# Products of an expert layer summed in two PSUM banks

## The chip, the cores and the metric

The kernel runs on one core of one Trainium2 chip. The metric is the device time of one execution in microseconds (us); lower is better. The engines are PE (TensorE: matrix products into PSUM; PEld is its weight load), DVE (VectorE), ACT (ScalarE), POOL (GpSimd) and SP (SyncE, which here issues DMAs). Each engine works off its own queue in order, and engines wait for each other through semaphores.

## The reference

```
attention:  for each of 768 steps:  y = r . state
            state = state * w - outer(state . a, b) + outer(v, k)        (4 x 8 heads of 40)
x = y as 3072 tokens x 320
mixture:    P = exp(x @ w_gate - max)           (3072 x 8)
            8 times:  P /= rows' sums;  P /= columns' sums;  P *= 3072 / 8
            for e in 0..7:  out += P[:, e] * (relu(x @ w1[e]) @ w2[e])   (w1: 320 x 1024, w2: 1024 x 320)
```

## The kernel before

The first 500 us compute the attention in chunks. The rest, which the change is about, is the mixture of experts, in 128 blocks. One block takes one expert, 768 of the 3072 tokens (four groups, held two at a time) and 256 of the 1024 hidden columns. Eight blocks in a row make up one expert for two token groups (two groups of four); all experts are gone through once for groups 0 and 1 and then, backwards, for groups 2 and 3. The PE works on fp32 numbers split into a high and a low part.

**First layer of a block (`layer1`).** The 2 x 2 block product is done with seven products instead of eight (`PROD`), each of 128 x 384 outputs and four matmuls (`product`). A product is written into one of two PSUM banks, `pl[0]` and `pl[1]`, that alternate: product j+2 can start only when product j has been read. In order they are 1, 2, 5, 6, 3, 7, 4 (`ORDER`). From them come two hidden tiles `sm0`, `sm1`, each with two halves of 384 tokens (`h1`, `h2`), through seven additions on VectorE (`add`), with two copies on ScalarE (`p1`, `p5`). Four times a half is then rectified by ScalarE (`relu`, high part `hh`), and VectorE computes the remainder max(sm, 0) - hh (`low`, low part `hl`). The last remainders of a block (`rest`) stand in the queues after the first product of the next block.

**Second layer (`layer2`).** Twelve units a block of three matmuls (128 x 320 outputs, into six banks `op0` to `op5`), which wait in `pend` and are put between the products of the next block: two after each of the first five products, one after each of the last two, three units behind (`LAG`). After the fourth block of a token group (`f == FP - 1`), `evac` moves each `op` bank out: a VectorE operation for most experts.

**Work beside it.** Each product is a slot. After each slot one step of `background` is put in the queues: `prep_w` splits the weights of a coming block (four ScalarE casts, nine GpSimd operations, lines 514 to 532), four preparations in each run of eight blocks; `prep_x` splits the tokens. `sinkhorn` computes the gate P in the first ten blocks: a step of it every few slots (`S_GAP`), with a matmul into one of the two `pl` banks each.

**Order.** Up to block 7 (`N_MAN = 8`) a scheduler with a timeline model orders the instructions; from block 8 on they stand in each queue as they were written.

Of the kernel before, what the change touches and what calls it, by code (L numbers as in the profile page):

```python
# [23 lines left out]
E, FF, DM = 8, 1024, 320  # L24
# [423 lines left out]
SC = 2  # L448
NT = 6
S_WAIT = 2  # L450
S_GAP = 5
LAG = 3
N_MAN = 8
D_WAIT = 6
ORDER = (1, 2, 5, 6, 3, 7, 4)
PROD = {1: (0, 0), 2: (1, 2), 3: (6, 1), 4: (2, 6), 5: (3, 3), 6: (4, 4), 7: (5, 5)}


# [1 line left out]
def body(ctx, tc, d, out):  # L460
    nc = tc.nc
# [5 lines left out]
    pmat = one.tile([128, 24, E], F32, name="pmat")  # L467
# [19 lines left out]
    pl = [ctx.enter_context(tc.tile_pool(name=f"pl{i}", bufs=1, space=bass.MemoryType.PSUM)) for i in range(2)]  # L487
# [77 lines left out]
                        op=ALU.subtract)  # L565
        yield

    def product(o, i, k, s):
        ia, ib = PROD[i]
        wh = whs[k % NWS][:, 640:2432].rearrange("r (i k m) -> r i k m", k=2, m=128)  # L570
        wl = wls[k % NWS][:, 640:1536].rearrange("r (i m) -> r i m", m=128)
        xh, xl = xch[s % SC], xcl[s % SC]
        ts = [(wh[:, ia, 0], xh[:, ib, 0]), (wh[:, ia, 0], xl[:, ib]), (wl[:, ia], xh[:, ib, 0]),
              (wh[0:96, ia, 1], xh[0:96, ib, 1])]
        for j, (w_, x_) in enumerate(ts):
            nc.tensor.matmul(o, lhsT=w_, rhs=x_, start=(j == 0), stop=(j == 3))  # L576

    def layer1(n, k, s):
        h1, h2 = slice(384, 768), slice(0, 384)
        v = nc.vector  # L580
        hh = hp.tile([128, 2, 768], F32R, name="hh")
        hl = hp.tile([128, 2, 768], F32R, name="hl")

        sm = [hp.tile([128, 768], F32, name=f"sm{i}", bufs=1) for i in range(2)]
        p1, p5, u2, u3 = (hp.tile([128, 384], F32, name=x, bufs=1) for x in ("p1", "p5", "u2", "u3"))

        def prod(i):
            j = (n + ORDER.index(i)) % 2
            o = pl[j].tile([128, 512], F32, name=f"p{i}", tag="pl")[:, 0:384]
            product(o, i, k, s)  # L590
            return o

        def add(out, x, y, eng=nc.vector):
            eng.tensor_tensor(out=out, in0=x, in1=y, op=ALU.add)  # L594

        def relu(f, h):
            nc.scalar.activation(out=hh[:, f, h], in_=sm[f][:, h], func=AF.Relu)  # L597

        def low(f, h):
            v.scalar_tensor_tensor(out=hl[:, f, h], in0=sm[f][:, h], scalar=0.0, in1=hh[:, f, h],  # L600
                                   op0=ALU.max, op1=ALU.subtract)

        nc.scalar.copy(out=p1, in_=prod(1))
        yield 2
        add(sm[0][:, h1], prod(2), p1)
        relu(0, h1)
        yield 2
        nc.scalar.copy(out=p5, in_=prod(5))
        low(0, h1)
        yield 2  # L610
        add(u2, prod(6), p1)
        yield 2
        add(p1, prod(3), p5)
        add(sm[0][:, h2], p1, u2)
        yield 2
        add(u3, prod(7), u2)
        relu(0, h2)
        add(sm[1][:, h2], p5, u3)
        yield 1
        add(sm[1][:, h1], prod(4), u3)  # L620
        low(0, h2)
        relu(1, h1)
        yield 1

        def rest():
            relu(1, h2)
            yield
            low(1, h1)
            low(1, h2)

        yield hh, hl, rest()

    def layer2(e, k, s, f, hh, hl):
        wh, wl = whs[k % NWS], wls[k % NWS]
        last = f == FP - 1

        def unit(h, i):
            cw = slice(h * DM, h * DM + DM)
            cs = slice(i * 128, i * 128 + 128)
            for j, (a, w_) in enumerate(((hh, wh), (hh, wl), (hl, wh))):  # L640
                nc.tensor.matmul(ops[i], lhsT=a[:, h, cs], rhs=w_[:, cw],  # L641
                                 start=(f == 0 and h == 0 and j == 0), stop=(last and h == 1 and j == 2))
            if last and h:
                evac(e, s, i)
            if h and i == 2 and s % SC == SC - 1 and k + NWS < NK and (s >= SC or e < E - 1):
                bg[0][0].append(prep_w(k + NWS))

        tiles = (3, 4, 5, 0, 1, 2)
        if last:
            return [partial(unit, h, i) for i in tiles for h in range(2)]  # L650
        return [partial(unit, h, i) for h in range(2) for i in tiles]

    def sinkhorn():
        v = nc.vector
        mxs = one.tile([128, 8], F32, name="mxs")
        mx, m1, mbs = mxs[:, 0:1], mxs[0:1, 1:2], mxs[:, 2:3]
        v.tensor_reduce(out=mx, in_=lg, op=ALU.max, axis=AX.XY)
        for _ in range(S_GAP):
            yield
        t = pl[0].tile([128, 512], F32, name="mp", tag="pl")[0:1, 0:128]  # L660
        nc.tensor.transpose(t, mx, ident)
        v.tensor_reduce(out=m1, in_=t, op=ALU.max, axis=AX.X)
        for _ in range(S_GAP):
            yield
        t = pl[1].tile([128, 512], F32, name="mb", tag="pl")[:, 0:1]
        nc.tensor.matmul(t, lhsT=ones[0:1], rhs=m1, start=True, stop=True)
        v.tensor_copy(out=mbs, in_=t)
        v.tensor_scalar(out=lg, in0=lg, scalar1=mbs, scalar2=None, op0=ALU.subtract)
        nc.scalar.activation(out=pmat, in_=lg, func=AF.Exp)
        for _ in range(S_GAP):  # L670
            yield
        rs = one.tile([128, 24], F32, name="rs")
        cl = one.tile([128, E], F32, name="cl")
        cs = one.tile([128, E], F32, name="cs")
        for i in range(8):
            v.tensor_reduce(out=rs, in_=pmat, op=ALU.add, axis=AX.X)
            v.tensor_scalar(out=rs, in0=rs, scalar1=EPS, scalar2=None, op0=ALU.add)
            v.reciprocal(out=rs, in_=rs)
            v.tensor_tensor(out=pmat, in0=pmat, in1=rs.unsqueeze(2).broadcast_to([128, 24, E]), op=ALU.mult)
            v.tensor_reduce(out=cl, in_=pmat.rearrange("p n e -> p e n"), op=ALU.add, axis=AX.X)  # L680
            for _ in range(S_GAP):
                yield
            t = pl[i % 2].tile([128, 512], F32, name="cp", tag="pl")[:, 0:E]
            nc.tensor.matmul(t, lhsT=ones, rhs=cl, start=True, stop=True)
            v.tensor_scalar(out=cs, in0=t, scalar1=EPS, scalar2=float(E) / NTOK, op0=ALU.add, op1=ALU.mult)  # L685
            v.reciprocal(out=cs, in_=cs)
            v.tensor_tensor(out=pmat, in0=pmat, in1=cs.unsqueeze(1).broadcast_to([128, 24, E]), op=ALU.mult)
            yield
        for i in range(NT):
            scale_acc(0, i)  # L690
            yield

    def scale_acc(s, i):
        nc.scalar.activation(out=acc[:, s * NT + i], in_=acc[:, s * NT + i], func=AF.Copy,
                             scale=pmat[:, s * NT + i, 0:1])

    def evac(e, s, i):
        n, m = s * NT + i, (s % SC) * NT + i
        if e == (0 if s < SC else E - 1):
            if s == 0:  # L700
                nc.scalar.copy(out=acc[:, m], in_=ops[i])
            else:
                nc.scalar.activation(out=acc[:, m], in_=ops[i], func=AF.Copy, scale=pmat[:, n, e:e + 1])
        else:
            nc.vector.scalar_tensor_tensor(out=acc[:, m], in0=ops[i], scalar=pmat[:, n, e:e + 1],
                                           in1=acc[:, m], op0=ALU.mult, op1=ALU.add)
# [16 lines left out]
    bg = [(deque(), deque()) for _ in range(2)]  # L723
    bg[0][0].extend(prep_w(k) for k in range(2, NWS))
    bg[1][0].extend(prep_x(1, u) for u in range(3))
    sink = sinkhorn()

    def background(slot):
        for new, act in bg:
# [8 lines left out]
    for n, (k, e, s, f) in enumerate(blocks):  # L738
# [92 lines left out]
```

## Time and profile before

| | |
|---|---|
| time of three runs | 1835.61 us median (1833.37 to 1836.29) |
| the profiled execution | 1835.4 us from the first to the last instruction |
| PE busy | 1732.4 us, 94% |
| DVE, ACT, POOL busy | 1360.2, 856.3, 873.2 us (74%, 47%, 48%) |
| 505 to 620 us (the first blocks) | PE busy 104.89 of 115 us, DVE 98.16 |
| 700 to 1800 us | PE busy 1100.00 of 1100 us, granted clock 1.00, DVE 816.16, ACT 444.91, POOL 518.43 |

The profiled execution lies 0.2 us below the median. A row of a group reads: line, engine, operation, output <- inputs by the program's names, shapes, count, busy us, mean ns of one, idle time before. A row of a timeline reads: start us, duration us, engine, line, operation, and in brackets an idle time before it with what ended it. Names like `p`, `sm`, `hl`, `hh` stand without their numbers there: `p<-p,p` on DVE is the sum of product 3 and the copy `p5`.

### The profile page before, as it was taken

How to read it: one execution, taken by the hardware profiler on the slowest of the kernel's cores; microseconds unless marked ns; L12 is line 12 of the kernel's file. 1: busy time of each engine (PE TensorE's matmuls, PEld its weight loads, DVE VectorE, ACT ScalarE, POOL GpSimd, SP SyncE). 2: the span in 40 equal slices, each digit the busy share in tenths (PEclk: the TensorE clock that was granted, in tenths of full speed). 3: DMA queues.
4: the chain of work that ended last, by engine and by line, in shares of the span. 5: the costliest groups of instructions: out<-in, count | busy, mean ns of one | idle time of the engine just before them, and what ended most of it. 6: DMA issues, size and time to landing. Idle time of an engine off the chain costs nothing.

```text
span 1835.4 us, 31595 instructions
## 1 busy us (share of the span) xinstructions
PE 1732.4 (94%) x11843; PEld 1703.2 (93%) x11843; DVE 1360.2 (74%) x2354; ACT 856.3 (47%) x1848; POOL 873.2 (48%) x849
## 2 busy tenths in 40 slices
PE   4479988999989999999999999999999999999999
PEld 4468888889889999999999999999999999999999
DVE  6876967866688868777776868977686877777676
ACT  6347767655743533434253434345343343425342
POOL 6545745631662626446281735007182644628160
PEclk8569999889899999999999999999999999999999
DMA  7567888875720101111020202201020111102001
GB/s 187 124 149 181 185 172 197 174 162 134 201 82 22 57 20 56 38 38 57 19 75 5 72 21 73 72 1 57 20 75 20 56 38 38 57 20 75 10 30 44
DMA packets 193303, 142.79 MB, mean 78 GB/s; under 512 B 141438, under 2 KB 170750, under 8 KB 193150
## 3 DMA queue, kind: packets, MB, share of 16 engines
q1 hardware_dynamic: 189469, 135.03, 28.4%
q10 hardware_dynamic: 3680, 5.74, 1.2%
q8 instruction: 94, 1.54, 0.3%
q14 instruction: 60, 0.48, 0.1%
HBM read 113.90 MB, written 26.82 MB: 77 GB/s over the span
## 4 chain that ended last, share of the span: by engine, by line
PE 79%; DVE 8%; DMA 5%; issue 2%; ACT 2%; POOL 2%; SPq 1%; DVEq 0%; POOLq 0%; ACTq 0%
PE op L641 36%; PE p L576 33%; DMA inp<-in_inp_dram 3%; PE xc L291 2%; PE pu L302 2%; PE av L283 1%; PE c L309 1%; PE ll L154 1%; DVE pr L188 1%; DMA td<-nd 1%; PE gp L256 1%; DVE q L119 1%; DVE hl L600 1%; PE op L261 1%; DVE sm L594 1%
## 5 line engine op out<-in xcount | busy, mean ns | idle before, releaser
L576 PE MATMUL p<-xch,wh 128*128 128x384 f32 (+1 forms) x1792 | 605.0, 339 | 5.9 <-DVE cs L685 1.8
L597 ACT ACTIVATE hh<-sm 128x384 fp32r<-128x384 f32 x512 | 269.4, 526 | 722.8 <-DVE sm L594 722.8
L641 PE MATMUL op<-wh,hh 128*128 128x320 f32 x1536 | 476.5, 311 | 2.1 <-ACT hh L597 2.1
L641 PE MATMUL op<-wl,hh 128*128 128x320 f32 x1536 | 474.2, 309 | 0.0
L641 PE MATMUL op<-wh,hl 128*128 128x320 f32 x1536 | 467.1, 310 | 2.1 <-DVE hl L600 2.1
L522 POOL TENSOR_TENSOR wl<-ws,wh 128x640 fp32r<-128x640 f32 x60 | 102.8, 1713 | 606.1 <-ACT wh L520 605.8
L600 DVE SCALAR_TENSOR_TENSOR hl<-sm,hh 128x384 fp32r<-128x384 f32 x512 | 372.6, 761 | 2.4 <-ACT hh L597 2.0
L576 PEld LDWEIGHTS p<-xch,wh 128*128 128x128 f32 (+1 forms) x1792 | 337.3, 188 | 9.8 <-DVE sm L594 3.3
L576 PE MATMUL p<-xcl,wh 128*128 128x384 f32 x896 | 302.6, 338 | 0.0
L576 PE MATMUL p<-xch,wl 128*128 128x384 f32 x896 | 301.8, 337 | 0.0
L641 PEld LDWEIGHTS op<-wh,hh 128*128 128x128 f32 x1536 | 289.9, 189 | 3.0 <-ACT hh L597 3.0
L641 PEld LDWEIGHTS op<-wl,hh 128*128 128x128 f32 x1536 | 290.7, 189 | 0.0
L641 PEld LDWEIGHTS op<-wh,hl 128*128 128x128 f32 x1536 | 286.8, 188 | 2.5 <-DVE hl L600 2.4
L594 DVE TENSOR_TENSOR sm<-p,u 128x384 f32<-128x384 f32 x384 | 234.7, 621 | 8.8
L576 PEld LDWEIGHTS p<-xcl,wh 128*128 128x128 f32 x896 | 168.7, 188 | 0.0
L576 PEld LDWEIGHTS p<-xch,wl 128*128 128x128 f32 x896 | 168.6, 188 | 0.0
L594 DVE TENSOR_TENSOR sm<-p,p 128x384 f32<-128x384 f32 x128 | 71.3, 557 | 128.5 <-PE p L576 72.1
L594 DVE TENSOR_TENSOR p<-p,p 128x384 f32<-128x384 f32 x128 | 71.1, 556 | 101.1 <-PE p L576 100.7
L594 DVE TENSOR_TENSOR u<-p,p 128x384 f32<-128x384 f32 x128 | 70.8, 553 | 57.0 <-PE p L576 55.7
L530 POOL TENSOR_TENSOR wl<-ss,wh 128x512 fp32r<-128x512 f32 x60 | 89.8, 1496 | 30.3 <-ACT wh L527 26.2
L154 PE MATMUL ll<-ab,kb 104*128 104x128 f32 x336 | 62.6, 343 | 39.5 <-POOL ab L149 14.8
L154 PEld LDWEIGHTS ll<-ab,kb 104*128 104x128 f32 x336 | 54.0, 243 | 45.1 <-POOL kb L142 27.0
(161 smaller groups left out, 2739.9 us busy)
## 6 DMA issues: line engine op xcount, KB each, us to landing
ws<-in_wts_dram SPq DMA_DIRECT2D x60, 832.0 KB
inp<-in_inp_dram SPq DMA_DIRECT2D x42, 419.2 KB
rb<-in_r_dram SPq DMA_DIRECT2D x48, 208.0 KB
ld<-lt ACTq DMA_DIRECT2D x40, 128.0 KB
gd<-g SPq DMA_DIRECT2D x48, 105.6 KB
gl<-gd SPq DMA_DIRECT2D x48, 105.6 KB
vz<-in_v_dram SPq DMA_DIRECT2D x48, 104.0 KB
xd<-y SPq DMA_DIRECT2D x24, 208.0 KB
```

The lines of the kernel that those rows point to most:

```text
L119: nc.vector.tensor_tensor_scan(out=qr.rearrange("r p t -> r (p t)"), data0=w65[:, 260:0:-1], data1=one65, initial=0.0, op0=ALU.mult, op1=A ...
L154: nc.tensor.matmul(ll[:, p], lhsT=kb[:, p], rhs=ab[:, p], start=True, stop=True)
L188: nc.vector.tensor_tensor(out=prv, in0=a.unsqueeze(2).broadcast_to([nu, n_c, n_r, n_k]), in1=m.unsqueeze(1).broadcast_to([nu, n_c, n_r, n_ ...
L291: nc.tensor.matmul(xc[h][:, p], lhsT=pp["sx"][:, p, h], rhs=f[:, p, h], start=True, stop=True)
L302: nc.tensor.matmul(pu[:, p], lhsT=tts[c][:, b * NP + p], rhs=x1[:, p], start=True, stop=True)
L522: g.tensor_tensor(out=wl[:, 0:640], in0=raw[:, 256:896], in1=wh[:, 0:640], op=ALU.subtract)
L530: g.tensor_tensor(out=lv[:, 3:7], in0=so[:, :, 0], in1=hv[:, 3:7, 0], op=ALU.subtract)
L576: nc.tensor.matmul(o, lhsT=w_, rhs=x_, start=(j == 0), stop=(j == 3))
L594: eng.tensor_tensor(out=out, in0=x, in1=y, op=ALU.add)
L597: nc.scalar.activation(out=hh[:, f, h], in_=sm[f][:, h], func=AF.Relu)
L600: v.scalar_tensor_tensor(out=hl[:, f, h], in0=sm[f][:, h], scalar=0.0, in1=hh[:, f, h], op0=ALU.max, op1=ALU.subtract)
L641: nc.tensor.matmul(ops[i], lhsT=a[:, h, cs], rhs=w_[:, cw], start=(f == 0 and h == 0 and j == 0), stop=(last and h == 1 and j == 2))
```

## The change

Products are taken in the order 1, 2, 6, 5, 7, 3, 4. Two banks `pa` and `pb` are taken once a block. Product 1 starts `pa`; products 6, 7 and 4 are added to it by the PE (`first=False`: no start flag), so that it holds in turn p1, u2 = p1 + p6, u3 = u2 + p7 and at last the whole h1 half of `sm1`. Product 2 uses `pb`, then product 5 starts it afresh and product 3 is added. ScalarE copies p1, u2, p5 and u3 out (four copies instead of two). VectorE does three additions instead of seven. The h1 half of `sm1` is never stored: ScalarE rectifies it from PSUM, and its remainder (`low(1, h1, pa)`, in `rest`) reads `pa` too. In blocks with f > 0, `layer2` takes the first six units in the order 0 to 5. `sinkhorn` does one iteration a block; its matmul goes into columns 384 to 511 of `pb`, ahead of the third product. All twelve `acc` tiles of the first expert are scaled later (`scale_acc`), and their `evac` is a plain copy.

```diff
-            nc.tensor.matmul(o, lhsT=w_, rhs=x_, start=(j == 0), stop=(j == 3))
+            nc.tensor.matmul(o, lhsT=w_, rhs=x_, start=(first and j == 0), stop=(j == 3),
+                             skip_group_check=not first)
...
-        nc.scalar.copy(out=p1, in_=prod(1))
+        product(pa, 1, k, s)
+        nc.scalar.copy(out=p1, in_=pa)
         yield 2
-        add(sm[0][:, h1], prod(2), p1)
-        relu(0, h1)
+        product(pb, 2, k, s)
+        add(sm[0][:, h1], pb, p1)
+        relu(0, h1, sm[0][:, h1])
         yield 2
-        nc.scalar.copy(out=p5, in_=prod(5))
-        low(0, h1)
+        sink_step("mm", banks[1][:, 384:512])
+        product(pa, 6, k, s, False)
+        nc.scalar.copy(out=u2, in_=pa)
+        low(0, h1, sm[0][:, h1])
         yield 2
-        add(u2, prod(6), p1)
+        product(pb, 5, k, s)
+        nc.scalar.copy(out=p5, in_=pb)
         yield 2
-        add(p1, prod(3), p5)
-        add(sm[0][:, h2], p1, u2)
+        product(pa, 7, k, s, False)
+        nc.scalar.copy(out=u3, in_=pa)
+        add(sm[1][:, h2], u3, p5)
+        relu(1, h2, sm[1][:, h2])
         yield 2
-        add(u3, prod(7), u2)
-        relu(0, h2)
-        add(sm[1][:, h2], p5, u3)
+        product(pb, 3, k, s, False)
+        add(sm[0][:, h2], pb, u2)
+        relu(0, h2, sm[0][:, h2])
+        low(1, h2, sm[1][:, h2])
         yield 1
-        add(sm[1][:, h1], prod(4), u3)
-        low(0, h2)
-        relu(1, h1)
+        product(pa, 4, k, s, False)
+        relu(1, h1, pa)
+        low(0, h2, sm[0][:, h2])
         yield 1
 
         def rest():
-            relu(1, h2)
+            low(1, h1, pa)
             yield
-            low(1, h1)
-            low(1, h2)
...
+        if f:
+            return [partial(unit, 0, i) for i in range(6)] + [partial(unit, 1, i) for i in tiles]
...
-            for _ in range(S_GAP):
-                yield
-            t = pl[i % 2].tile([128, 512], F32, name="cp", tag="pl")[:, 0:E]
+            t = (yield "mm")[:, 0:E]
...
-        for i in range(NT):
-            scale_acc(0, i)
-            yield
+        for i in range(SC * NT):
+            scale_acc(i)
+            yield "slot"
```

What stands in VectorE's queue from block 18's products to the start of block 19's, before (`p3`, `p7`, `p4` are products in PSUM; TENSOR_TENSOR is an addition, SCALAR_TENSOR_TENSOR on `hl` a remainder; `p1`, `p5`, `u2`, `u3`, `sm` at the inputs are in SBUF):

```order
L594 TENSOR_TENSOR p1_7725<-p3_7792,p5_7726 128x384
L594 TENSOR_TENSOR sm0_7723<-p1_7725,u2_7727 128x384
L594 TENSOR_TENSOR u3_7728<-p7_7807,u2_7727 128x384
L594 TENSOR_TENSOR sm1_7724<-p5_7726,u3_7728 128x384
L594 TENSOR_TENSOR sm1_7724<-p4_7819,u3_7728 128x384
L600 SCALAR_TENSOR_TENSOR hl_7722<-sm0_7723,hh_7721 128x384
L594 TENSOR_TENSOR sm0_7833<-p2_7852,p1_7835 128x384
L600 SCALAR_TENSOR_TENSOR hl_7722<-sm1_7724,hh_7721 128x384 x2
```

And the same place now (`p0_7601` is the bank `pa` and `p1_7602` the bank `pb` of block 18, `p1_7705` is `pb` of block 19, the same physical bank as `p0_7601`):

```order
L589 TENSOR_TENSOR sm1_7596<-u3_7600,p5_7598 128x384
L589 TENSOR_TENSOR sm0_7595<-p1_7602,u2_7599 128x384
L595 SCALAR_TENSOR_TENSOR hl_7594<-sm1_7596,hh_7593 128x384
L595 SCALAR_TENSOR_TENSOR hl_7594<-sm0_7595,hh_7593 128x384
L595 SCALAR_TENSOR_TENSOR hl_7594<-p0_7601,hh_7593 128x384
L589 TENSOR_TENSOR sm0_7698<-p1_7705,p1_7700 128x384
```

Before, the last operation that reads a bank of block 18 is the addition of `p4`, and the two remainders of `sm1` come after block 19's first addition. Now all three late remainders stand in one row ahead of that addition, and the last of them reads the bank.

ScalarE's queue at the same place, before (a CAST on `wh` belongs to `prep_w`):

```order
L608 COPY p5_7726<-p5_7764 128x384
L524 CAST wh3_5627<-ss_7742 128x512
L527 CAST wh3_5627<-ss_7742 128x512
L597 ACTIVATE hh_7721<-sm0_7723 128x384
L597 ACTIVATE hh_7721<-sm1_7724 128x384
```

And now:

```order
L611 COPY p5_7598<-p1_7602 128x384
L522 CAST wh3_5627<-ss_7615 128x512
L614 COPY u3_7600<-p0_7601 128x384
L592 ACTIVATE hh_7593<-sm1_7596 128x384
L525 CAST wh3_5627<-ss_7615 128x512
L592 ACTIVATE hh_7593<-sm0_7595 128x384
L592 ACTIVATE hh_7593<-p0_7601 128x384
```

The fourth cast has moved behind the copy of u3 and the first of three Relu operations.

More of the change, by code (lines that the diff above doesn't have):

```diff
@@ L450 @@
 S_WAIT = 2
-S_GAP = 5
 LAG = 3
@@ L454 @@
 D_WAIT = 6
-ORDER = (1, 2, 5, 6, 3, 7, 4)
 PROD = {1: (0, 0), 2: (1, 2), 3: (6, 1), 4: (2, 6), 5: (3, 3), 6: (4, 4), 7: (5, 5)}
@@ L566, in prep_x, with product @@
         yield
-    def product(o, i, k, s):
+    def product(o, i, k, s, first=True):
         ia, ib = PROD[i]
@@ L585, in layer1 @@
         p1, p5, u2, u3 = (hp.tile([128, 384], F32, name=x, bufs=1) for x in ("p1", "p5", "u2", "u3"))
[L587 to L597, printed above, removed]
@@ L599, in low, with add, relu @@
-        def low(f, h):
-            v.scalar_tensor_tensor(out=hl[:, f, h], in0=sm[f][:, h], scalar=0.0, in1=hh[:, f, h],
+        banks = [pl[(n + j) % 2].tile([128, 512], F32, name=f"p{j}", tag="pl") for j in range(2)]
+        pa, pb = (t[:, 0:384] for t in banks)
+        def add(out, x, y):
+            v.tensor_tensor(out=out, in0=x, in1=y, op=ALU.add)
+        def relu(f, h, x):
+            nc.scalar.activation(out=hh[:, f, h], in_=x, func=AF.Relu)
+        def low(f, h, x):
+            v.scalar_tensor_tensor(out=hl[:, f, h], in0=x, scalar=0.0, in1=hh[:, f, h],
@@ L657, in sinkhorn @@
         v.tensor_reduce(out=mx, in_=lg, op=ALU.max, axis=AX.XY)
-        for _ in range(S_GAP):
-            yield
-        t = pl[0].tile([128, 512], F32, name="mp", tag="pl")[0:1, 0:128]
+        t = (yield "mm")[0:1, 0:128]
         nc.tensor.transpose(t, mx, ident)
         v.tensor_reduce(out=m1, in_=t, op=ALU.max, axis=AX.X)
-        for _ in range(S_GAP):
-            yield
-        t = pl[1].tile([128, 512], F32, name="mb", tag="pl")[:, 0:1]
+        t = (yield "mm")[:, 0:1]
         nc.tensor.matmul(t, lhsT=ones[0:1], rhs=m1, start=True, stop=True)
@@ L669, in sinkhorn @@
         nc.scalar.activation(out=pmat, in_=lg, func=AF.Exp)
-        for _ in range(S_GAP):
-            yield
+        yield "slot"
         rs = one.tile([128, 24], F32, name="rs")
@@ L680, in sinkhorn @@
             v.tensor_reduce(out=cl, in_=pmat.rearrange("p n e -> p e n"), op=ALU.add, axis=AX.X)
-            for _ in range(S_GAP):
-                yield
-            t = pl[i % 2].tile([128, 512], F32, name="cp", tag="pl")[:, 0:E]
+            t = (yield "mm")[:, 0:E]
             nc.tensor.matmul(t, lhsT=ones, rhs=cl, start=True, stop=True)
@@ L687, in sinkhorn, with scale_acc, sink_step @@
             v.tensor_tensor(out=pmat, in0=pmat, in1=cs.unsqueeze(1).broadcast_to([128, 24, E]), op=ALU.mult)
-            yield
-        for i in range(NT):
-            scale_acc(0, i)
[L691 to L695, printed above, removed]
+            yield "slot"
+        for i in range(SC * NT):
+            scale_acc(i)
+            yield "slot"
+    def scale_acc(i):
+        nc.scalar.activation(out=acc[:, i], in_=acc[:, i], func=AF.Copy, scale=pmat[:, i, 0:1])
+    def sink_step(at, psum=None):
+        if slot > S_WAIT and waits[0] == at:
+            try:
+                waits[0] = sink.send(psum)
+            except StopIteration:
+                waits[0] = None
     def evac(e, s, i):
@@ L699, in evac @@
         if e == (0 if s < SC else E - 1):
-            if s == 0:
+            if s < SC:
                 nc.scalar.copy(out=acc[:, m], in_=ops[i])
@@ L725, in body @@
     bg[1][0].extend(prep_x(1, u) for u in range(3))
-    sink = sinkhorn()
+    sink, waits = sinkhorn(), ["slot"]
     def background(slot):
@@ L751, in body @@
             background(slot)
-            if slot > S_WAIT:
-                next(sink, None)
+            sink_step("slot")
         rest = h[2]
```

## The prediction

> **What bounds the kernel now.** I read the stretches first, then the PE's waits, then the groups, then the timeline of single blocks. The stretches (us; each engine's busy time with its count):
>
> ```profile
> 505.00:620.00 115.00, 104.89 (x631) 99.82 (x630) 98.16 (x188) 52.70 (x106) 54.23 (x49) 0.97 0.16 49
> 620.00:1800.00 1180.00, 1180.00 (x7416) 1179.47 (x7415) 876.01 (x1486) 478.38 (x941) 556.56 (x480) 1.00 0.13 43
> ```
>
> Columns after the length: PE, PEld, DVE, ACT, POOL, then the granted clock. From 620 us on the PE has no gap and full clock, so relief for VectorE is worth nothing there; any wait that the PE gets is added to the time in full. Only the first blocks have gaps; the PE's waits from 505 to 620 us (total, times, longest):
>
> ```profile
> PE op L641 <- DVE hl L600: 2.1, 1, 2.1
> PE op L641 <- ACT hh L597: 2.1, 3, 1.1
> PE p L576 <- DVE cs L685: 1.8, 1, 1.8
> PE p L576 <- DVE sm L594: 1.7, 3, 1.0
> PE p L576 <- DVE u L594: 1.6, 3, 0.8
> PE p L576 <- DVE mxs L662: 0.5, 1, 0.5
> ```
>
> These are 9.8 us, and the longest is followed by a half clock:
>
> ```profile
> 523.00:530.00 7.00, 6.50 (x21) 0.52 0.22 89
> ```
>
> That costs 0.48 x 7.0 = 3.4 us. What a faster VectorE could win is at most 9.8 + 3.4 = 13 us.
>
> **The operations' prices** (mean ns before the last bar):
>
> ```profile
> L600 DVE SCALAR_TENSOR_TENSOR hl<-sm,hh 128x384 fp32r<-128x384 f32 x512 | 372.6, 761 | 2.4 <-ACT hh L597 2.0
> L705 DVE SCALAR_TENSOR_TENSOR acc<-op,pmat,acc 128x320 f32<-128x320 f32 x168 | 91.3, 543 | 4.5 <-PE op L641 4.4
> L594 DVE TENSOR_TENSOR u<-p,u 128x384 f32<-128x384 f32 x128 | 70.9, 554 | 23.9 <-PE p L576 23.3
> L597 ACT ACTIVATE hh<-sm 128x384 fp32r<-128x384 f32 x512 | 269.4, 526 | 722.8 <-DVE sm L594 722.8
> L608 ACT COPY p<-p 128x384 f32<-128x384 f32 x128 | 61.1, 478 | 29.5 <-PE p L576 28.5 <-PE op L641 0.7
> L522 POOL TENSOR_TENSOR wl<-ws,wh 128x640 fp32r<-128x640 f32 x60 | 102.8, 1713 | 606.1 <-ACT wh L520 605.8
> L530 POOL TENSOR_TENSOR wl<-ss,wh 128x512 fp32r<-128x512 f32 x60 | 89.8, 1496 | 30.3 <-ACT wh L527 26.2
> ```
>
> The remainder's mean of 761 hides two cases:
>
> ```profile
> L600 DVE SCALAR_TENSOR_TENSOR hl<-sm,hh x512: 495/552/1936, 508.6 to 1826.1; 128x384 fp32r<-128x384 f32 x171
> ```
>
> Median 0.55 us, longest 1.94. What lies behind it is seen in block 18. VectorE, operations with both inputs in SBUF, and one that waited for a product:
>
> ```profile
> 712.14 1.43 DVE L594 TENSOR_TENSOR sm<-p,u 128x384 f32<-128x384 f32 x1
> 715.25 1.18 DVE L600 SCALAR_TENSOR_TENSOR hl<-sm,hh 128x384 fp32r<-128x384 f32 x1
> 716.99 0.56 DVE L594 TENSOR_TENSOR sm<-p,p 128x384 f32<-128x384 f32 x1 [0.56 <-PE p L576]
> ```
>
> GpSimd at the same time:
>
> ```profile
> 712.13 1.02 POOL L525 TENSOR_TENSOR wl<-ws,wh 128x384 fp32r<-128x384 f32 x1
> 713.23 1.22 POOL L528 TENSOR_TENSOR wh<-ws,wh 32x384 fp32r<-32x384 f32 x1
> 714.52 1.49 POOL L530 TENSOR_TENSOR wl<-ss,wh 128x512 fp32r<-128x512 f32 x1
> 716.09 1.50 POOL L532 TENSOR_TENSOR wh<-ss,wh 32x512 fp32r<-32x512 f32 x1
> ```
>
> L525 ends at 713.15, the addition 0.42 later (713.57); L530 ends at 716.01, the remainder again 0.42 later (716.43). So a VectorE operation with two SBUF inputs that starts while GpSimd is in an operation waits for that operation's end and then takes 0.42 us. Operations with one input in PSUM keep 543 to 554 ns whatever GpSimd does (their means above). The Trainium skill ("SBUF — State Buffer", Who interferes with whom) states an exclusive lock of this kind for two SBUF inputs; were it wrong and the mean of 761 true of every remainder, the walk below would end before the PE needs the bank, with no stall and about 1831 us, and the trace's two 0.42 speak for the lock.
>
> GpSimd's share, in stretches of 11 us:
>
> ```profile
> 693.00:704.00 11.00, 10.61 (x10) 1.00 0.23 77
> 704.00:715.00 11.00, 10.61 (x10) 1.00 0.24 79
> 715.00:726.00 11.00, 6.21 (x6) 1.00 0.22 77
> 726.00:737.00 11.00, 0.00 (x0) 1.00 0.01 1
> ```
>
> It is all but full for four blocks and then idle for four. L522 runs once a preparation: 60 less 4 for the first blocks is 56, in 14 runs of four; the first run starts while the scheduler's order still holds, so I count 55 blocks (13 runs of four, and three).
>
> **The new path.** When the PE needs the banks is seen in the same block (sixth product, seventh, the next block's first and second, and the second's last matmul):
>
> ```profile
> 712.17 0.34 PE L576 MATMUL p<-xch,wh 128*128 128x384 f32 x1
> 713.32 0.34 PE L576 MATMUL p<-xch,wh 128*128 128x384 f32 x1
> 714.46 0.34 PE L576 MATMUL p<-xch,wh 128*128 128x384 f32 x1
> 716.03 0.34 PE L576 MATMUL p<-xch,wh 128*128 128x384 f32 x1
> 716.56 0.34 PE L576 MATMUL p<-xch,wh 96*128 96x384 f32 x1
> ```
>
> Count from the sixth product: 0, 1.15, 2.29, 3.86. A reader of a product starts 0.43 after its last matmul began (716.56, then 716.99), so 0.96 after its start. The next block's second product goes into the old `pa`; it must wait for `low(1, h1, pa)`, which stands behind the sum of product 3, `low(1, h2)` and `low(0, h2)`. Back-to-back operations start 0.47 apart:
>
> ```profile
> 690.49 0.54 DVE L705 SCALAR_TENSOR_TENSOR acc<-op,pmat,acc 128x320 f32<-128x320 f32 x1
> 690.96 0.54 DVE L594 TENSOR_TENSOR u<-p,p 128x384 f32<-128x384 f32 x1
> ```
>
> *GpSimd idle:* sum 0.96 to 1.52; first remainder from 1.43; Relu 1.55 to 2.08, second remainder 2.1 to 2.65; third, after its own Relu (1.15 + 0.96 + 0.53 = 2.64), 2.67 to 3.23. Needed at 3.86: no stall, and none with one `evac` (0.47) in between.
>
> *GpSimd busy, first block of a run:* the fourth cast now stands behind a Relu, so L530 starts late. First remainder 1.43 to 1.98 undisturbed; L530 then takes 1.49, to 3.47; second remainder ends 3.89; third 3.81 to 4.37.
>
> *The other three:* GpSimd is some 2 us later. The addition for the h2 half of `sm1` (two SBUF inputs) waits out L525, its Relu follows, and the first remainder starts at about 1.65 to 1.9 in L528, which ends near 2.05: done 2.47. L530 then holds until 3.96, second remainder 4.38, third 4.3 to 4.86. An `evac` in between falls into the wait for L530.
>
> How the PE goes on after such a wait:
>
> ```profile
> 554.13 0.56 DVE L594 TENSOR_TENSOR u<-p,p 128x384 f32<-128x384 f32 x1
> ```
>
> ```profile
> 554.74 0.44 PE L576 MATMUL p<-xch,wh 128*128 128x384 f32 x1 [0.65 <-DVE u L594]
> 555.02 0.34 PE L576 MATMUL p<-xcl,wh 128*128 128x384 f32 x1
> ```
>
> It starts 0.05 after the reader's end, and its next matmul comes after 0.28 instead of 0.17: 0.1 more. The first block of a run loses 4.37 + 0.05 - 3.86 + 0.1 = 0.66 us, each other one 4.86 + 0.05 - 3.86 + 0.1 = 1.15 us. Sum: 13 x 0.66 + 42 x 1.15 = **57 us**. Bounds a block: nothing, where GpSimd itself waits at that place, as in the walk for GpSimd idle; 1.74 us, where the first remainder starts with L528's 1.22 and the second with a 1.49 (1.43 + 1.22 + 0.42 + 1.49 + 0.42 - 0.09 + 0.56 + 0.05 - 3.86 + 0.1). So 0 to 96 us; I take 57, from the order in which L525, L528 and L530 stand.
>
> **The other parts.** VectorE loses four additions a block, 128 x 4 x 0.55 = 282 us of its 1360; worth nothing after 620 us. In the first blocks 8 x 4 x 0.55 = 18 us of its 98 go, and the gate's matmul no longer takes a bank of its own. Of the 13 us I take 5 as won, since the same three remainders at a block's end stand in the way there too, with GpSimd busy for 54 of 115 us (bounds: 13 won, 6 lost). The two more copies (2 x 0.478 a block) lie in ScalarE's idle time: 478 of 1180 us busy plus 113; the bank copied last, u3's, is free 1.15 + 1.57 - 0.96 - 0.48 = 1.28 us before product 4 needs it. The six more scalings and the PE's accumulation cost nothing: as many matmuls as before, three of four accumulated already. The new order of units: unit 0 reads the second remainder only after the product that waits for the third. `prep_x` in blocks 59 to 70 puts two operations of 0.42 us ahead of the third remainder, six times, which takes up the 0.58 us to spare there (3.86 - 0.05 - 3.23): 0 to 4 us, I take 1.
>
> ```profile
> 1153.74 0.42 DVE L548 TENSOR_TENSOR xt<-xs 128x256 f32<-128x256 f32 x1
> ```
>
> **Sum:** 1835.4 + 57 + 1 - 5 = 1888 us; the profiled execution is 0.2 below the median, which changes nothing.
>
> **Rivals.** *Faster:* the late remainders are released in time after all (for instance GpSimd's operations fall elsewhere, since VectorE takes two fewer of its locks a block), and the first blocks win 5: 1831 us. Against it: it needs 0.5 us off in the best and 1.05 in the usual block; it decides when the chain's end falls below 3.86. *No change:* both the stalls and the gain are small, 1835. *Half clock after each stall:* the wait of 2.1 us was followed by 7 us at 0.52; if each of 55 stalls did that, 3.4 x 55 = 187 more, 2075 us. Against it: the waits of up to 1.8 us after 541 us left the clock at 1.00:
>
> ```profile
> 541.00:613.00 72.00, 68.67 (x418) 1.00 0.10 32
> ```
>
> The Trainium skill ("TensorE: Matmul & The Clock Gate", A second HAM failure mode) tells of a kernel whose PE micro-idles while cycling through PSUM banks and falls to half clock again and again; by that page this rival would be the likely one, and the trace here does not agree for waits of about 1 us.
>
> **How the numbers follow.** The held bank 0.84; faster 0.10; no change 0.04; half clock 0.02. A run of this kernel tells about 0.2% from no change, 3.7 us. The likeliest case gives 1888. Within it the time runs from 9 us of stalls (1840) to 94 (1925), close to its bounds; outside lie faster, same, half clock and its tails, together 2 in 10. So faster 0.10, same 0.04, slower 0.86.
>
> **What would show it.** Right: from 620 us on the PE's waits list the line of the products behind the remainder's line, some 55 times, about 1 us each, only in blocks where GpSimd is busy; blocks without it stay at 10.2 us; the clock stays 1.00; DVE's busy time falls by less than 282 us, for the remainders get longer. Wrong: no PE wait after 620 us (the chain was walked too slowly), or waits behind ScalarE's copies instead, or a clock below 1.00.

## The result, and the profile after

| | before | after |
|---|---|---|
| median of four runs | 1835.95 us (1833.37 to 1837.01) | 1854.33 us (1848.66 to 1855.24) |
| the profiled execution, first to last instruction | 1835.4 us | 1853.5 us |
| PE, DVE busy | 1732.4, 1360.2 us | 1749.9, 1064.1 us |
| ACT, POOL busy | 856.3, 873.2 us | 986.3, 830.8 us |

The ratio is 1.0087 with a 95% interval of [1.0068, 1.0106]: the change makes the kernel some 16 us slower by the ratio, 18 by the medians and the two traces. The direction and the place were forecast; the stalls were forecast four times too large.

The stretches of after (columns as in the prediction: PE, PEld, DVE, ACT, POOL, granted clock):

```profile
505.00:620.00 115.00, 107.35 (x656) 101.55 (x655) 79.20 (x149) 59.17 (x121) 51.45 (x50) 0.97 0.16 49
527.00:534.00 7.00, 5.68 (x19) 5.39 (x20) 3.88 (x7) 1.85 (x4) 6.84 (x8) 0.52 0.07 30
620.00:1800.00 1180.00, 1177.85 (x7307) 1162.54 (x7306) 593.86 (x1008) 592.76 (x1168) 517.53 (x481) 1.00 0.13 42
```

The PE still reads as busy from 620 us on, but it gets through 7307 matmuls where it got through 7416. At 1180 / 7416 = 0.159 us each, the 109 missing ones are 17 us. So the loss lies here, at full clock. The PE's busy time hides it: its rows last 0.31 us or more and start 0.15 us apart, so that a step of 0.30 leaves no gap between them; the weight loads (PEld, 1162.54 of 1180) show it. What the weight loads and the matmuls waited for in this stretch (us in total, times, longest):

```profile
PEld p L574 <- DVE hl L595: 17.4, 60, 0.9
```

```profile
PE p L574 <- DVE hl L595: 1.7, 4, 0.6
```

L574 is the line of the products and L595 that of the remainders: a product waits for the remainder that reads its bank, as forecast, though 60 times at 0.29 us each rather than 55 times at about 1 us. The first products of four blocks that follow each other while GpSimd is busy:

```profile
768.81 0.34 PE L574 MATMUL p<-xch,wh 128*128 128x384 f32 x1
779.26 0.34 PE L574 MATMUL p<-xch,wh 128*128 128x384 f32 x1
789.71 0.34 PE L574 MATMUL p<-xch,wh 128*128 128x384 f32 x1
800.16 0.34 PE L574 MATMUL p<-xch,wh 128*128 128x384 f32 x1
```

They lie 10.45 us apart; blocks without GpSimd keep 10.18. By the starts of all blocks in the two traces, the 18.1 us between the spans divide so: 0.6 before the first product, 1.3 from there to block 8, 16.1 in blocks 8 to 126, nothing behind. Blocks 8 to 126 take 19.7 us beyond 10.18 us each, before 3.5. Of the 16.1 us more, 13.7 stand in thirteen runs of four blocks (as a rule 10.45, 10.45, 10.45, 10.43), 0.5 in blocks 8 to 11 and 1.9 in blocks 61 to 67, where `prep_x` works.

The end of one such block (sixth product at 766.53), VectorE first:

```profile
767.43 0.56 DVE L589 TENSOR_TENSOR sm<-p,u 128x384 f32<-128x384 f32 x1 [0.35 <-PE p L574]
767.91 0.55 DVE L595 SCALAR_TENSOR_TENSOR hl<-sm,hh 128x384 fp32r<-128x384 f32 x1
768.61 1.41 DVE L595 SCALAR_TENSOR_TENSOR hl<-sm,hh 128x384 fp32r<-128x384 f32 x1 [0.16 <-ACT hh L592]
769.95 0.54 DVE L595 SCALAR_TENSOR_TENSOR hl<-p,hh 128x384 fp32r<-128x384 f32 x1
```

GpSimd:

```profile
765.66 1.01 POOL L526 TENSOR_TENSOR wh<-ws,wh 32x384 fp32r<-32x384 f32 x1
768.30 1.31 POOL L528 TENSOR_TENSOR wl<-ss,wh 128x512 fp32r<-128x512 f32 x1 [1.63 <-ACT wh L525]
769.69 1.48 POOL L530 TENSOR_TENSOR wh<-ss,wh 32x512 fp32r<-32x512 f32 x1
```

The PE, from the last unit ahead of the next block's second product:

```profile
770.25 0.31 PE L642 MATMUL op<-wh,hl 128*128 128x320 f32 x1
770.55 0.44 PE L574 MATMUL p<-xch,wh 128*128 128x384 f32 x1
770.82 0.34 PE L574 MATMUL p<-xcl,wh 128*128 128x384 f32 x1
```

The second remainder starts at 768.61 with both inputs in SBUF, finds GpSimd in its operation until 769.61 and ends at 770.02, 0.41 later. The third, on the bank, is through at 770.49, and the PE starts at 770.55: 0.15 later than the usual step of 0.15 from 770.25, and the next matmul follows after 0.27 instead of 0.17. That makes 0.25 us. Each of the steps of the forecast's chain is there; only its lengths differ.

VectorE's remainders by their inputs (min, median, max in ns):

```profile
L595 DVE SCALAR_TENSOR_TENSOR hl<-sm,hh x384: 544/558/1532, 511.5 to 1842.5; 128x384 fp32r<-128x384 f32 x192
L595 DVE SCALAR_TENSOR_TENSOR hl<-p,hh x128: 542/549/559, 516.2 to 1843.0; 128x384 fp32r<-128x384 f32 x128
```

Of the 128 that read PSUM none takes over 559 ns. The bank's reader itself is never held up; it stands behind one that is.

The first blocks, the three longest items of what the PE waited for from 505 to 622 us:

```profile
PE p L662 <- DVE sm L589: 3.0, 1, 3.0
PE p L574 <- ACT p L599: 1.8, 1, 1.8
PE p L574 <- DVE sm L589: 1.6, 2, 0.9
```

The waits there, 7.5 us in all, replace 9.8 us of before, and with the longest, which ended at 528.14, again go 7 us at half clock (the row at 527 above). L662 is the gate's matmul, which waits for the sum that still reads the bank it writes into.

### The profile page after: what moved, and what is told of

Its sections match the earlier page's. It is cut to its first block, busy times and chain, and to the rows that moved or that the text cites. A ratio compares the mean times of both kernels' runs of the same rounds, so it can differ in the third digit from the quotient of the medians.

```text
span 1853.5 us, 31595 instructions
## 1 busy us (share of the span) xinstructions
PE 1749.9 (94%) x11843; PEld 1705.0 (92%) x11843; DVE 1064.1 (57%) x1842; ACT 986.3 (53%) x2110; POOL 830.8 (45%) x849
## 3 DMA queue, kind: packets, MB, share of 16 engines
q8 instruction: 94, 1.54, 0.4%
## 4 chain that ended last, share of the span: by engine, by line
PE 75%; DVE 8%; DMA 7%; ACT 3%; issue 2%; POOL 2%; SPq 1%; ACTq 0%; DVEq 0%; POOLq 0%
PE op L642 35%; PE p L574 33%; DMA inp<-in_inp_dram 3%; PE xc L291 2%; PE pu L302 1%; PE c L309 1%; DVE hl L595 1%; PE av L283 1%; DVE pr L188 1%; PE ll L154 1%; DMA ld<-lt 1%; DVE sm L589 1%; DMA td<-nd 1%; POOL ab L148 1%; POOL kb L142 1%
## 5 line engine op out<-in xcount | busy, mean ns | idle before, releaser
L574 PE MATMUL p<-xch,wh 128*128 128x384 f32 (+1 forms) x1792 | 610.7, 343 | 6.2 <-DVE hl L595 2.2
L520 POOL TENSOR_TENSOR wl<-ws,wh 128x640 fp32r<-128x640 f32 x60 | 95.6, 1593 | 627.4 <-ACT wh L518 600.9
L592 ACT ACTIVATE hh<-sm 128x384 fp32r<-128x384 f32 x384 | 201.6, 525 | 310.5 <-DVE sm L589 310.4
L574 PEld LDWEIGHTS p<-xch,wh 128*128 128x128 f32 (+1 forms) x1792 | 337.3, 188 | 25.4 <-DVE hl L595 18.4
L595 DVE SCALAR_TENSOR_TENSOR hl<-sm,hh 128x384 fp32r<-128x384 f32 x384 | 284.6, 741 | 79.7 <-ACT hh L592 68.9
L574 PE MATMUL p<-xcl,wh 128*128 128x384 f32 x896 | 302.8, 338 | 0.6 <-DVE xcl L554 0.6
L574 PE MATMUL p<-xch,wl 128*128 128x384 f32 x896 | 302.3, 337 | 0.0
L589 DVE TENSOR_TENSOR sm<-u,p 128x384 f32<-128x384 f32 x128 | 74.5, 582 | 327.3 <-ACT u L614 323.5
L574 PEld LDWEIGHTS p<-xcl,wh 128*128 128x128 f32 x896 | 168.9, 189 | 0.9 <-DVE xcl L554 0.9
L574 PEld LDWEIGHTS p<-xch,wl 128*128 128x128 f32 x896 | 168.6, 188 | 0.0
L611 ACT COPY p<-p 128x384 f32<-128x384 f32 x128 | 61.7, 482 | 125.2 <-PE p L574 120.5
L614 ACT COPY u<-p 128x384 f32<-128x384 f32 x128 | 61.7, 482 | 110.8 <-PE p L574 110.7
L707 DVE SCALAR_TENSOR_TENSOR acc<-op,pmat,acc 128x320 f32<-128x320 f32 x168 | 91.5, 545 | 36.3 <-PE op L642 36.3
L528 POOL TENSOR_TENSOR wl<-ss,wh 128x512 fp32r<-128x512 f32 x60 | 82.7, 1379 | 64.8 <-ACT wh L525 44.8
L599 ACT COPY p<-p 128x384 f32<-128x384 f32 x128 | 61.7, 482 | 79.1 <-PE p L574 78.7
```

The lines of the kernel that those rows point to most:

```text
L520: g.tensor_tensor(out=wl[:, 0:640], in0=raw[:, 256:896], in1=wh[:, 0:640], op=ALU.subtract)
L528: g.tensor_tensor(out=lv[:, 3:7], in0=so[:, :, 0], in1=hv[:, 3:7, 0], op=ALU.subtract)
L574: nc.tensor.matmul(o, lhsT=w_, rhs=x_, start=(first and j == 0), stop=(j == 3), skip_group_check=not first)
L589: v.tensor_tensor(out=out, in0=x, in1=y, op=ALU.add)
L592: nc.scalar.activation(out=hh[:, f, h], in_=x, func=AF.Relu)
L595: v.scalar_tensor_tensor(out=hl[:, f, h], in0=x, scalar=0.0, in1=hh[:, f, h], op0=ALU.max, op1=ALU.subtract)
```

## The experiments

The letters of the theories are those of the expectations: A is the forecast's own mechanism, B the accumulation in two banks with ScalarE's copies and casts, C a sharing of bandwidth in place of a lock, D the gate's matmul as the cause of the first blocks' long wait, E the token preparation as its cause. The runs of one group shared the runs of the kernel before: e1 to e4 stand against 1837.47 us (25 runs), e5 to e8 against 1837.87 (26), e9 and e10 against 1839.87 (12). Two kernels of one group whose intervals overlap are not told apart by them.

**e1, the bank read first.** The two last remainders of a block change places: the one that reads `pa` now stands ahead of the second of the two that read SBUF.

```diff
         product(pa, 4, k, s, False)
         relu(1, h1, pa)
-        low(0, h2, sm[0][:, h2])
+        low(1, h1, pa)
         yield 1
 
         def rest():
-            low(1, h1, pa)
+            low(0, h2, sm[0][:, h2])
             yield
```

> The changed kernel with the two last remainders of a block exchanged: the one that reads the PSUM bank is taken straight after its Relu, the one of sm0's second half afterwards, ahead of the next block's first sum. Theory A, the bank is held by a queue of remainders that a GpSimd operation lengthens: from 620 us on the PE no longer waits, the blocks beside GpSimd's work come back from 10.45 to 10.18 us, about 15 us less than the changed kernel, 1838 to 1841. Theory B, the time goes into the accumulation in two banks and ScalarE's four copies and later casts, wherever the remainders stand: unchanged within 2 us, 1854.

Measured: 1836.43 us over 10 runs, ratio 0.9991 [0.997, 1.0012], a little less than A expected. VectorE in the same block (sixth product at 765.26):

```profile
766.63 0.55 DVE L595 SCALAR_TENSOR_TENSOR hl<-sm,hh 128x384 fp32r<-128x384 f32 x1
767.82 0.56 DVE L595 SCALAR_TENSOR_TENSOR hl<-p,hh 128x384 fp32r<-128x384 f32 x1 [0.64 <-ACT hh L592]
768.30 0.55 DVE L595 SCALAR_TENSOR_TENSOR hl<-sm,hh 128x384 fp32r<-128x384 f32 x1
```

GpSimd beside it:

```profile
767.03 1.31 POOL L528 TENSOR_TENSOR wl<-ss,wh 128x512 fp32r<-128x512 f32 x1 [1.63 <-ACT wh L525]
768.41 1.59 POOL L530 TENSOR_TENSOR wh<-ss,wh 32x512 fp32r<-32x512 f32 x1
```

The wait from 620 us on:

```profile
PEld p L574 <- DVE hl L595: 1.2, 2, 0.7
```

The remainder from PSUM takes its 0.56 us while GpSimd is in its operation (767.03 to 768.34). It ends 3.1 us after the sixth product's start instead of 4.0, 60 waits become 2, and blocks 8 to 126 take 3.3 us beyond 10.18 us each, as in the kernel before. The whole loss of those blocks, those with `prep_x` included, thus hangs on the order of the two last remainders on VectorE; A holds, and B, by which this order would not have won the time back, is out.

**e2, no GpSimd work** after the first four preparations.

```diff
+        if k >= NWS:
+            nc.scalar.copy(out=wh[:, 640:1408], in_=raw[:, 896:1664])
...
+            return
```

> The changed kernel without GpSimd's part of the weight preparations from the fifth on: the casts and loads stay, the low parts of those weights are left as they were. Theory A: no VectorE operation is held up by GpSimd, the last remainder ends 0.6 us before the bank is needed, and the blocks take 10.18 us: 1838 to 1841. Theory B (accumulation, copies, casts): unchanged within 2 us, 1854.

Measured: 1835.73 us over 10 runs, 0.9991 [0.997, 1.0013], a little less than expected. The stretch, and the remainders in it (L607 here):

```profile
620.00:1800.00 1180.00, 1179.67 (x7407) 1177.85 (x7406) 536.01 (x1021) 598.91 (x1179) 0.00 (x0) 1.00 0.13 43
```

```profile
L607 DVE SCALAR_TENSOR_TENSOR hl<-sm,hh x346: 547/558/560, 622.6 to 1795.2; 128x384 fp32r<-128x384 f32 x173
```

With the order of the changed kernel and GpSimd silent, no remainder takes over 560 ns and the matmuls are back (7407). It takes both, GpSimd's operation and the order, to lose the 13.7 us of the thirteen runs. The 1.9 us of blocks 61 to 67 stay without GpSimd (six waits for a remainder from 620 to 1800 us): there VectorE's own queue with `prep_x` in it is enough.

**e3, one operation of GpSimd split in two.**

```diff
-        g.tensor_tensor(out=lv[:, 3:7], in0=so[:, :, 0], in1=hv[:, 3:7, 0], op=ALU.subtract)
+        g.tensor_tensor(out=lv[:, 3:5], in0=so[:, 0:2, 0], in1=hv[:, 3:5, 0], op=ALU.subtract)
+        g.tensor_tensor(out=lv[:, 5:7], in0=so[:, 2:4, 0], in1=hv[:, 5:7, 0], op=ALU.subtract)
```

> The changed kernel with the GpSimd operation that meets the second remainder (four matrices of 128 columns, 1.3 to 1.4 us) split into two of two matrices each, the same work in total. Theory A with an exclusive lock held for one whole operation: the second remainder waits for about 0.75 us instead of 1.3, the chain ends 0.5 us earlier, which is more than the 0.15 us that the PE waits: no wait after 620 us, 1838 to 1842. Rival C, GpSimd and VectorE share the port in proportion, so that GpSimd's total work counts: unchanged within 2 us, 1854.

Measured: 1841.83 us over 10 runs, 1.002 [1.0003, 1.0038]. VectorE's last two remainders in the first block of a run, and GpSimd's two operations beside them:

```profile
763.29 0.85 DVE L596 SCALAR_TENSOR_TENSOR hl<-sm,hh 128x384 fp32r<-128x384 f32 x1 [0.16 <-ACT hh L593]
764.07 0.54 DVE L596 SCALAR_TENSOR_TENSOR hl<-p,hh 128x384 fp32r<-128x384 f32 x1
```

```profile
762.91 0.82 POOL L529 TENSOR_TENSOR wl<-ss,wh 128x256 fp32r<-128x256 f32 x1 [0.55 <-ACT wh L525]
763.81 1.50 POOL L531 TENSOR_TENSOR wh<-ss,wh 32x512 fp32r<-32x512 f32 x1
```

L529 ends at 763.73 and the remainder at 764.14, again 0.41 later: the hold ends with the single operation, and VectorE gets in between two of them. That is a lock for an operation and not a sharing of bandwidth, under which the split would have changed nothing, so C is out. More than half of the loss in the thirteen runs is won back: they take 5.7 us beyond 10.18 us a block, and 14.3 in the changed kernel. The first and third blocks of a run take 10.18 us, the second 10.5, the fourth 10.25. The expectation of no wait at all held for half the blocks only. In the second block of the run above, an `evac` stands ahead of the sum of product 3 and another between the two remainders, and the addition ahead of them takes 1.27 us beside GpSimd's L526; the sum starts 1.54 us after the sixth product instead of 0.90 as in the block shown before.

**e4, the gate later.** The gate starts one block later (after slot 9 instead of 2), with its scalings three a slot.

```diff
-S_WAIT = 2
+S_WAIT = 9
...
-            yield "slot"
+            if i % 3 == 2:
+                yield "slot"
```

> The changed kernel with the gate started one block later (first step after slot 9 instead of 2; the scalings three to a slot). Theory D, the first blocks win nothing because the gate's first matmul, now in the second bank, waits 3.0 us for the sum that reads that bank, and half clock follows: these 3 us and up to 3.4 us behind them go, 1848 to 1851. Rival E, the first blocks are held by the token preparation on VectorE beside GpSimd, and the gate only stood in that gap: within 1.5 us of 1854.

Measured: 1852.54 us over 4 runs, 1.0086 [1.0059, 1.0114]. The waits from 505 to 620 us:

```profile
PE p L574 <- DVE sm L589: 4.7, 3, 3.0
PE p L574 <- ACT p L599: 1.8, 1, 1.8
```

The time alone would not tell D from E, for 1.0086 has an interval of 0.5%. The trace does: the gate's first matmul now comes at 538.2 us instead of 528.1, and the wait of 3.0 us is still there without it, on the product that comes in its place (it ends at 524.40). D falls: the gate's matmul stood in the gap and did not make it. E fits, by the time and by VectorE's queue (its rows stand in the next section).

**e5, GpSimd's longest operation done twice**, for the preparations after the first four.

```diff
-        g.tensor_tensor(out=wl[:, 0:640], in0=raw[:, 256:896], in1=wh[:, 0:640], op=ALU.subtract)
+        for _ in range(2 if k >= NWS else 1):
+            g.tensor_tensor(out=wl[:, 0:640], in0=raw[:, 256:896], in1=wh[:, 0:640], op=ALU.subtract)
```

> The changed kernel with GpSimd later: from the fifth weight preparation on, its longest operation (128 x 640, 1.57 us alone) is done twice with the same result. Theory A with the walk of the prediction: GpSimd now is some 2 us later in a block, so that the first remainder too meets an operation, as I had assumed for three blocks of four; the blocks beside GpSimd's work take 10.18 + 0.9 to 1.2 instead of 10.45, 30 to 48 us more than the changed kernel, 1884 to 1902. If the PE's loss does not hang on where GpSimd stands (theory B): unchanged within 3 us, 1854.

Measured: 1907.4 us, one run, without an interval. What the weight loads waited for from 620 us on:

```profile
PEld p L575 <- POOL wh L527: 30.8, 37, 1.1
PEld p L575 <- POOL wl L524: 18.2, 20, 1.0
PEld p L575 <- DVE hl L596: 12.8, 19, 1.3
```

The time lies 5 us above what was expected, and most of it has another reason: GpSimd's weights themselves come too late (49 of the 62 us here), in the second to the fourth block of a run. The first block of each of the thirteen runs, though, waits for a remainder only (13 waits, 10.4 us in all), and it is the case that the forecast had for three blocks of four. There (sixth product at 768.89), GpSimd first and VectorE's three remainders behind it:

```profile
769.67 1.21 POOL L527 TENSOR_TENSOR wh<-ws,wh 32x384 fp32r<-32x384 f32 x1
771.22 1.29 POOL L529 TENSOR_TENSOR wl<-ss,wh 128x512 fp32r<-128x512 f32 x1 [0.34 <-ACT wh L526]
```

```profile
770.60 0.70 DVE L596 SCALAR_TENSOR_TENSOR hl<-sm,hh 128x384 fp32r<-128x384 f32 x1
771.53 1.40 DVE L596 SCALAR_TENSOR_TENSOR hl<-sm,hh 128x384 fp32r<-128x384 f32 x1 [0.24 <-ACT hh L593]
772.85 0.55 DVE L596 SCALAR_TENSOR_TENSOR hl<-p,hh 128x384 fp32r<-128x384 f32 x1
```

L527 ends at 770.88 and the first remainder 0.42 later; L529 ends at 772.51 and the second again 0.42 later. The third ends 4.51 us after the sixth product, where the forecast's walk had 4.86, and the block takes 10.99 us, 0.81 beyond 10.18 where the walk had 1.15. So the forecast's second case exists and costs 0.8 us where it occurs.

**e6, the gate's part alone**, in the kernel before: one iteration a block, in free columns of product 2's bank.

```diff
-            t = pl[i % 2].tile([128, 512], F32, name="cp", tag="pl")[:, 0:E]
+            t = (yield "mm")[:, 0:E]
...
+        sink_step("mm", side[0])
```

> The kernel before with the gate's part of the change alone: one iteration a block, its matmul in the free columns of product 2's bank, twelve scalings; the first layer as before. If the gate's old banks cost the first blocks something (the waits of 1.8 and 0.5 us listed before): 2 to 4 us less than before. If these waits only change their names (theory E): within 2 us of before. No stall after 620 us in either.

Measured: 1846.42 us over 7 runs, 1.0042 [1.0019, 1.0064]; the first blocks take 110.4 us from the first product to block 8, 107.0 before. The PE's waits there:

```profile
PE p L576 <- DVE u L599: 7.5, 11, 1.6
PE op L647 <- DVE hl L605: 3.5, 1, 3.5
```

Neither expectation holds: beside the old first layer the denser gate costs some 8 us by the ratio. VectorE still has its seven additions there, and the gate's operations come on top, closer together; that this is the reason is likely from the waits, but not shown.

**e7 and e8, e1 with fewer blocks under the scheduler.**

For e7:

```diff
-N_MAN = 8
+N_MAN = 3
```

For e8:

```diff
-N_MAN = 8
+N_MAN = 1
```

> The kernel of e1 with the written order from block 3 on instead of block 8. With VectorE relieved, the first blocks could do without the scheduler: blocks 3 to 7 take 10.2 us instead of about 10.7, 2 to 3 us less than e1, 1833 to 1835. If the token preparation beside them needs the scheduler's order: 2 to 10 us more than e1.

> The same with the written order from block 1 on. If the scheduler's order costs the 20 us that block 1 takes: 3 to 8 us less than e1, 1829 to 1834. If block 1 is held by the token preparation and the end of the attention, whose matmuls can then no longer be mixed in: the same or up to 10 us more.

Measured: e7 1838.23 us over 12 runs, 1.0000 [0.9983, 1.0018]; e8 1833.32 over 12, 0.9972 [0.9953, 0.9992]. Three blocks win nothing. With one, the time lies just below that of the kernel before; the interval overlaps those of e1 and e7, so that a gain over the scheduler's order is not shown.

**e9, the same step on the kernel before** (`N_MAN = 8` to `1` alone).

> The kernel before with the written order from block 1 on, as in e8, and nothing else. If e8's gain over before comes from the written order alone: 0.2 to 0.4% less than before here too. If the written order in the first blocks works only with VectorE relieved (seven additions and four remainders a block stand beside the token preparation here): 0.2 to 1% more than before.

Measured: 1846.59 us over 6 runs, 1.0047 [1.0029, 1.0064].

```profile
505.00:620.00 115.00, 99.64 (x575) 95.19 (x573) 88.65 (x174) 43.97 (x90) 42.23 (x40) 0.91 0.14 42
```

In the kernel before, the written order gets 575 matmuls through here, the scheduler's 631. So the written order costs the kernel before 0.5% and the kernel of e1 nothing. That VectorE's additions make the difference was expected; the two kernels differ in the gate too, and no run here parts the two.

**e10, e8 with the gate one block later**, its scalings three a slot (the edit of e4 on e8).

> The kernel of e8 with the gate started one block later, as in e4. If the waits of 5.7 us that e8's first blocks still have behind VectorE's first sums hang on the gate: 2 to 5 us less than e8. If they hang on the token preparation: within 1.5 us of e8, 0.2 to 0.4% under before.

Measured: 1830.28 us over 7 runs, 0.996 [0.9945, 0.9974], below both kernels.

```profile
505.00:620.00 115.00, 108.92 (x681) 106.17 (x681) 81.44 (x149) 63.49 (x130) 57.30 (x54) 0.99 0.18 56
```

```profile
PE p L574 <- DVE sm L589: 4.6, 2, 3.4
```

681 matmuls in the stretch, 631 before; the clock is 0.99. Whether the later gate itself wins anything stays open: the ratio of e8, from another group, is 0.9972 and the intervals overlap, so that neither expectation is told from the other. Against the change as made (1.0087) its edits (the order of the remainders, `N_MAN`, the later gate) are worth 1.3% together, of which the order alone is 1.0% (e1).

## Why the prediction was right in sign and wrong in size

**The mechanism held.** The forecast was a PE that waits at the second product of a block for the third remainder, in blocks with GpSimd at work, at full clock. All of it is in the rows above; e1 (order alone), e2 (GpSimd alone) and e3 (length of the hold alone) each take the loss in the thirteen runs away or more than halve it. The measured 1854.3 us lie 34 below the forecast of 1888.

**The term that was mis-sized is the held bank**, 57 us; the thirteen runs of four blocks hold 13.7, and blocks 8 to 11, of which three were counted in, 0.5. Two steps of the walk failed.

*"L530 then takes 1.49, to 3.47"* (first block of a run). 1.49 was the group's mean, and a mean of an operation that is itself held up. GpSimd's rows with 512 columns show it: they take 1.31 us with 0.15 us of VectorE's remainder still to run and 1.59 with 0.44 to run (e1), and 1.48 with 0.33 to run (769.69 above). All three give some 1.28 us of work, if the lock is handed over some 0.13 us ahead of the end that the row of VectorE shows. And it did not wait for the remainder's end at 1.93 us after the sixth product: it started at 1.77, when its cast was done. So it ended at 3.08 instead of 3.47, the second remainder at 3.49 instead of 3.89, the third at 3.96 instead of 4.37. Of 0.66 us, 0.25 remain. Where the slack is 3.86 us and the chain 4.4, an error of 0.4 in the chain is most of the stall.

*"The other three: GpSimd is some 2 us later."* L526 starts 0.9 us later against the sixth product than in the first block, and the operation behind it no later at all. The second block of the run, whose sixth product starts at 776.98, on GpSimd and then on VectorE:

```profile
777.00 1.30 POOL L526 TENSOR_TENSOR wh<-ws,wh 32x384 fp32r<-32x384 f32 x1
778.64 1.42 POOL L528 TENSOR_TENSOR wl<-ss,wh 128x512 fp32r<-128x512 f32 x1 [0.34 <-ACT wh L525]
```

```profile
778.35 0.55 DVE L595 SCALAR_TENSOR_TENSOR hl<-sm,hh 128x384 fp32r<-128x384 f32 x1
```

L526, which the walk had in the first remainder's way until 2.05 us, is through at 1.32, and the remainder starts at 1.37. GpSimd then idles 0.34 us for ScalarE's cast, so L528 ends at 3.08 in this block too. The cast behind the Relu, rather than GpSimd's own backlog, sets the time of the lock, and all four blocks lose the same 0.25 to 0.27 us instead of 0.66 and 1.15. L526 misses the remainder by 0.05 us. The walk, which had it 0.7 us late, came out on the other side of a threshold worth 0.9 us a block, and multiplied that by 42: some 38 of the 43 us that are missing. Where the first remainder is held (e5), the block loses 0.81 us, so that this second case was sized too large as well. The forecast's lower bound (nothing, if GpSimd waits at that place) came near: GpSimd does wait there, but its next operation still meets the second remainder.

**The first blocks**, 5 us won by the forecast: 1.3 us lost between the traces (107.0 to 108.3 us from the first product to block 8), the waits falling by 2.3 us. Kernels with the same or nearly the same first blocks (e1 to e5) gave 104.1 to 106.0, one trace each, so neither the 5 nor the 1.3 is told from nothing. The longest wait comes from VectorE's queue, where the sum that reads the bank stands behind the splits of `prep_x` (four in a row, 6.3 us; the last of them and the sum):

```profile
526.26 1.24 DVE L557 TENSOR_TENSOR xch<-xs,xch 32x384 fp32r<-32x384 f32 x1
527.53 0.56 DVE L589 TENSOR_TENSOR sm<-p,p 128x384 f32<-128x384 f32 x1
```

Four additions fewer did not shorten that row of splits, and the half clock behind it stayed as before. That the gate by itself makes the first blocks dearer (e6) was not foreseen, beside the old first layer at least; it was counted as a small gain.

**`prep_x`**: 1 us taken, 0 to 4 as bounds, 1.9 measured, and there without GpSimd too (e2), as the walk had it.

**What was taken to cost nothing:** ScalarE's copies (ACT 986.3 us, up by 130) stand in no wait of the PE from 620 us on. In the first blocks one wait of 1.8 us stands behind the copy of p1 (L599), which the kernel before has too. The PE's accumulation costs next to nothing: e1 gets 7410 matmuls through from 620 to 1800 us, before 7416.

**VectorE's time** was to fall by less than 282 us, for longer remainders, and fell by 296. The remainders got no longer on the whole: the mean of the 384 with two SBUF inputs is 741 ns, where the 512 of before had 761, and the 128 that now read PSUM take 550.

**The rivals.** The half clock after each stall is out: 60 waits of up to 0.9 us from 620 us on (up to 0.6 on the matmuls' own rows), with a granted clock of 1.00. (The row of the forecast that ends at 613 us holds waits of up to 1.0 us; the one of 1.8 ended at 615.66, and the clock was 1.00 there too.) The Trainium skill ("TensorE: Matmul & The Clock Gate", A second HAM failure mode) tells of a kernel whose short waits between groups of matmuls bring the half clock again and again. The changed kernel's trace does not agree for its waits, but that of e5 does in part. In the third block of each run of e5 the PE waits twice for weights, up to 0.68 and 0.83 us and 1.3 us apart, and in four of the thirteen the clock then fell for 3.4 us, for instance:

```profile
1056.20:1059.60 3.40, 3.40 (x14) 3.40 (x13) 0.56 (x1) 1.36 (x3) 3.24 (x4) 0.50 0.76 250
```

Those four blocks take 13.8 us, where the others of their kind take 12.2. So the rival was wrong for this kernel's waits, and came true in part for somewhat longer ones in pairs. "Faster" was 0.16 us a block away: with the chain below 3.86 us it is e1, which measures no change.

**Open:** which part of the first blocks' time belongs to the gate in the changed kernel, whether the written order or the later gate wins anything by itself on the kernel of e1, and from which wait on the clock falls.

## What to carry to other kernels

An operation that gives back a bank the PE waits for belongs ahead of those in its queue that can be held up by another engine, above all when it cannot be held up itself: here that was worth 16 us for two lines moved. A walk along a chain that ends near its deadline should use durations of undisturbed operations, for a group's mean already holds the waits that the walk adds again. And where a small shift decides between two cases, multiply neither by the number of blocks before it is clear which engine's release sets the start.

## What the runs showed of the hardware

- The lock between GpSimd and VectorE goes both ways. GpSimd's operation of 512 columns took 1.31 us with 0.15 us left of VectorE's remainder and 1.59 with 0.44 left (e1), and VectorE's remainder ended 0.41 us after GpSimd's operation (769.61 and 770.02; 763.73 and 764.14). That whoever comes first holds the ports for a whole operation, and that a VectorE operation with one SBUF input, outside its 2-port modes, stays clear, is what the Trainium skill says ("SBUF — State Buffer", Who interferes with whom), and the rows agree.
- With one input in PSUM the same VectorE operation took 542 to 559 ns in 128 of 128 cases, in the middle of GpSimd's operations too.
- After a wait for a bank the PE started 0.06 us behind the reader's end, and its second matmul came 0.27 instead of 0.17 us after the first: a wait of 0.15 us costs 0.25.
- With one wait of 3.0 us in the first blocks went 7 us at a granted clock of 0.52, while 60 waits of up to 0.9 us later left it at 1.00. In e5 pairs of waits of up to 0.68 and 0.83 us, 1.3 us apart, brought 3.4 us at 0.50 in four of thirteen cases.
